# A gated recurrence and a PReLU layer on one core: gate factors folded, two chains made tasks of their own, and a new order of all instructions

## The chip, the core and the metric

The kernel runs on one core of a Trainium2 chip. The core has five engines with a queue of instructions each: TensorE (PE, with its weight loads as PEld), VectorE (DVE), ScalarE (ACT), GpSimd (POOL) and SyncE (SP), which here issues all transfers between the chip's memory (DRAM) and the core's memory. An engine takes its instructions in the order in which the program lists them; between engines, semaphores make one wait for another. The metric is the time of one execution on the device in microseconds (us); lower is better.

## The reference

Two layers follow each other. The first is a linear recurrence with a complex gate for each of 4 batches and 8 heads, over 768 tokens, with 48 channels; the second takes its output as 3072 tokens of 384 values.

```python
mag = np.sqrt(a_re * a_re + a_im * a_im)
scale = np.minimum(mag, 0.999) / (mag + 1e-06)
a_re_n, a_im_n = (a_re * scale, a_im * scale)
for t in range(S):
    ar, ai = (a_re_n[:, :, t, :, None], a_im_n[:, :, t, :, None])
    new_re = ar * S_re - ai * S_im
    new_im = ar * S_im + ai * S_re
    kv = np.einsum('bhd,bhe->bhde', k[:, :, t], v[:, :, t])
    S_re, S_im = (new_re + kv, new_im)
    y[:, :, t] = np.einsum('bhd,bhde->bhe', q[:, :, t], S_re)
...
h = x @ w_in
g = np.maximum(h, 0.0) + alpha * np.minimum(h, 0.0)
return (g @ w_out).astype(np.float32)
```

In the second layer w_in is 384 x 2048 and w_out 2048 x 384. All arithmetic of the kernel is in 32-bit floats; w_in, w_out arrive in 64 bits and are narrowed in the kernel.

## The kernel before, in words

The recurrence is not run token by token. A gate value is split into its magnitude, capped at 0.999 (the "decay"), and a number of length one (the "phase"). The products of phases up to each token turn q and k, so that inside a chunk of 128 tokens only real decays are left.

**Gates (`gates`, L229 to L516).** The work is cut into nine groups: the first batch's six chunks as 1, 2 and 3, each later batch as 3 and 3. A group of three chunks is a tile of 128 rows with six rows of 1152 columns, called x, c, f, d, e, y; the first group has 384 columns and is computed in halves, the second has 768. The steps for one group are: load a_re into x and a_im into y (L255); squares on ScalarE and their sum on VectorE (L263 to L269); reciprocal roots on ScalarE with a correction step on VectorE (L272 to L289); ScalarE's scaling of the magnitude c (L291); two products that turn x and y into the unit number (L363); the capped decay, written over rows d and e (`dec`, L380); copies that put the unit number into an order by place in blocks of eight tokens (`unit_numbers`, L344 to L358: the imaginary part, the real part and the negated imaginary part on ScalarE). Then the decay tree (L391 to L397): six levels of products of neighbouring decays, from 64 per chunk down to 2, the small ones on GpSimd from the fourth group on; then the transfer of the decays to a DRAM buffer, `decs` (L401). Then the running products of the unit numbers (`product`, L412 to L419: two VectorE instructions, L416 and L418, per step, in three rounds within blocks of eight, blocks of sixty-four and between those), one Newton step that brings their length back to one (L486 to L494), and the final product of each token's number with its block's (L507, L510), which overwrites the decay rows and is sent to a DRAM buffer, `phs` (L502, L512).

**Chunks (`unit`, L724 to L953).** There are 24. For each one q and k (`KQ`), the phases (`PP`), the decays with their tree (`T`) and v (`V`, `VL`) are loaded. VectorE turns q and k (L742, L744) and multiplies them by decays level after level (L797). TensorE makes the scores of six levels (`ps_lv`, L759), from copies that ScalarE puts in order (L820, L836). Then follow two transposes of k (L868), the update of the state from k and v (`ps_kv`, L880; state `St`, L916 on ScalarE and L918 on VectorE), the outputs inside the chunk (`ps_y`, L900), and those from the state (L930). ScalarE copies the sum out (L944), and it goes to DRAM (L949) and back as columns (`xT`, L962).

**The second layer.** `features` (L970) multiplies by w_in on TensorE (L978), ScalarE and VectorE make the PReLU (L985, L987); `outputs` (L992) multiplies by w_out (L997). The last three groups of tokens use a form with seven products in place of eight (L1097, L1172). The 64-bit weights are narrowed in `to_f32` by all of ScalarE (L588 to L592), GpSimd (L596) and VectorE (L598, L600).

**What sets the order.** Each of these is a Python generator, a task, that yields once ahead of each piece of work. The string `ORDER` at the top has one letter per step; `Plan.run` resumes the task of that letter and so writes its next instruction (or few) into the queues of the engines. The order of every queue is therefore fixed by that string, within the order inside each task. Buffers are single or few: V and VL one each, PP one, T two, KQ three, the gate tile two.

Of the kernel before, what the change touches and what calls it, by code (L numbers as in the profile page):

```python
# [9 lines left out]
F32 = mybir.dt.float32  # L10
# [8 lines left out]
P = 128  # L19
# [11 lines left out]
    "AAJMMAABAJAAAAAAAAAAAAAAAAAAAAMMMBJMAAAAAAAAAAKANAOAAAABAAANAAAKANNNABAMAJNBKOAKBOOKAABMAKABAAALOAAB"  # L31
    "LAKNOLNAALBOLANNAALBBLAAKBAKBBAKABABKMAAKBAAOAABAAAAAABABBABAAABAOOABABMANAAAAAAABAAAKBABNABBNBNOBOC"
    "BOCBJNNBLBOJBBOONBBNBBOCBBPBCBPPJLJMJCLKBNBCMBCJBPLBPCBOPPJCPBBBPOBPPBBNBPBBNNBBCPPMLPBLBBPLKBPKBCCC"
    "PLOKBKBPKBBBBCBPKCOOPKBPPPCPBPBCBPPPPBBPBCBBPBBPBBPBPCBPMPBCCBCBPNBKLCCNLCNPCPOCOJDCNDPPPJCOJNNCCCNJ"
    "OCNOOLCNOPCNKOMNNCPQPDJCQDLCDNQPPDQQQLCDQDKQQMCLNDQDOKPQQMODQLOOJQJDKQJDOLCQnOJOLDDJQNJOQLQLOOoLoDDC"
    "QLoQRQoLQQLQooooQQCoQDKNJooooRoMQoQCRCCoooooQoRDQQQCODDCONNCooRQRLoDCLRoMoLoCRRLCoooooCJoRDKCRKooooo"
    "RCDoRQLCDLCoooCoRKoOLCDJCQDCCoLDCRRDDCooooooLCQCooCLCoCoCoLCLCCCLCRCCLCKOCRCRLoCooCRRRCRRoRRCoCRCQQC"
    "CRCQCCoRKCRQRQQCQOORRoRCCQCCooRRCNQDoLoDLoNoDNoooNDoEDNNoEOJoDJRJDRLoooooDDoLDRRRLDRRLRDNDNEJDJSDDRo"
    "oJDESDEDSRDRJESSnJSoLESDoLoLODJSSJDSDLLTSDJoELoooooSSSDLoLooooJSSoDDDoSEDLoooSToSoJooJSSSDoSSDSSoooo"
    "ooSTSDETooooTToSEEoEDoooooSDToSEDTSESSSSDooLDTLoooLEEDSLToLSLoooooDLELoTJDSSSDoooooTTSDSESSSLoDooooo"  # L40
    "SEEDTLLoTKoooooDDDToTEJLDDDDoooooTEUJTDKoDoooKTToDoLoToooTLoUoDJoTLToooToEJoDonooToDEoDTKoUoDJooToUo"
    "EoEUTUEoETEDDDJTooUooDoUUoDooToToTTDoLoLoULoLDULLoooUUoDoLooooDoULoLoELooooLoUULoTLUTLJoooooFUEUoETT"
    "TUUUUTTTUooooTToUETUUFEoUEooooEoUVoUEoooooVVKJJUUEUUEUUoFooLEFLoUoLEUFJVUELoVJoUJooooVJEoFVEJEVoEUoo"
    "oUUUEVoEUoLoVVLEoooEoLEoVEJooooJVEWoFEnVVLoVELoLoooEoKVVEoELVEoJFooooJWoVoVFooWLooLVVEEWoLWVoLWVEFJV"
    "VVJEooVoVoooEKoWKoJEoooVEWWooVWoVoEFWVVVEVVEWELWEELooFEELoWLEoEoLoWWLVLoWEEEEVLLooooooLWEWLEoLEFELEK"
    "FFVVVooWooLooVVVVVFFFVLXKEoEWooooooEWWEEWWJoWWJoooWoEJWoWJoFJWoEWFFWWWWoEoELoLEoJoLoEoFXEooooFooooXo"
    "ooooKXWXLXFWoXoGGXLoXooooJWoLXoLWoFWXoXWFXWoFWXFWWoWXoXFFoFLoXoGFJFnGooooXXoJFoFLoLXXXXLGFLoooooXLFX"
    "XXoGoLFGFLoooooooFXoooGFoJoYJXoJFoJXFGKoooXFYFXoXFYJFooooGXXXYoYXLYFooLXFYFKoLoYoYLXXFZLFXLoXYXFLoXX"
    "XoooYXoFGLGFYYLoYGoFJoYFYJoooFoFZoLFoJoYJGKooooFJGYFYLooYYYLoJYYZGLLFoooooZLoFGYZYZoYZYKJFZZooooYFoZ"
    "YoYFGZYYFYFFYYFZFLFZFFLoYLoooZLooLoFFFFFYFZLFZYYYLFoZLYYFLYoooFZYLaZFLoFoooZZZZoYZZLZoGYFFLLoooZoZGo"  # L50
    "LGoFZJoZFFFGJoooooFooZFFZZFZZZGLoonoFLooLaoFoLoooaJoLoZoaJGoLZooaJaGoaoHoLZZLaaZoHGGoGZGZGGaZLGaLooo"
    "ooaZGaLoaJoZaZaooooGJoHaooHGoooaoaGLaHoooLoGLaaJaHoaJaaJoooooHoGbaoaGHoooaoGaobbJKHoaGaoaoaGaaHoLKoG"
    "JoboLGobLGoLGoooGbLoHGHbLboJbHoGJLaoLbbGLooooGoGHobLGaLaHbLGbabLaabaaGoLaooooLGbboGoGHbGooooJbGbGGKo"
    "bbboJobJbGGbcbbJobGGoooboGcbooooGbGoHbGbGcbbbLGcGLoooGbLcGHcGGJoboJcoLJGGGobLGccLGoobKcbLobHLbobbLoc"
    "obHoGHGdbLGHooooccocGoJoJHoooLcocdJooLconJHLoooocLcHoccccoccLGoJdcGGooocodHocHoHdHoHcGGGcoooGooocGGc"
    "GccccodGLLoooGcodooooLoddJoooLocdoLoIHIoHLdooooLHooLHdcoLdcoLdcLocJHcocddoHoHooKcoooILdocoLHoIHdcdLH"
    "LddoIKdooooJdoIddJoddKdHoHooodoHdoIoHedHHodeHIdddodoHLeHLoLoIHodLHoHLHeIHoLdLoooeeJHeHLoLdddHoooeeoH"
    "JHdedHLoJooooeIoLIeLeoeJddoLHoooLeeoLoHdIHeodJoHIHoooeeoJeeeeoeJeoeIJeoenJHIHoooeJIoeooHeHoHfeeoeHfe"
    "eoLLHoHHJHoHHeHoLfeoLILJHHHHofLooooofeLHfeHfLeHKoeIeLoKffLeHoooooefHeoeLgIIfogJLooooIoooffofoHJILooo"
    "ooHLffoJIoJfHHoooooKHofofJooLfffffofKoJgooHofgIoooggoIHIofofHIoIIoofoHKfooHofogfffoffggoLHLoLogoLoHI"  # L60
    "oLgoooILofnoIfgLgLgLfffoLggJoLgfKoooofooooIgLogfooLfIfofggggggogoohgogIhhLJJJIIhIooooogogoIIoogggggg"
    "oLILogoJIoJgIohJgIILgIgooohLIIgoJgIoIghILhIoIghILoLhhIooooIoIhIoJoLihILJooohhohLoLohLohoooLioJIIoLho"
    "LoJiJooohohooJhhiohhihJhihnoIIIhIoIIhIIIIooohIoIhIioIhihhhhhIihoLihLLLohhhLIIIIIiooooLohhiILiIoLiILo"
    "hLoooiiIoLohihohoLIoooILiIiLoLiiiiiioJioJioIIiIoooioiojoioIiiijIiiJooLojLoJoIoJoLjoooiLoIioLojIjiiiI"
    "jiiooooojjooooLojLiiJoooojLopoLjojiiLoooJjoLoojjJLojLLoooooJojLojooJjjjjjJojjJopjojookkkoojojooojjkj"
    "jojjokLkoLkLokJokoLokLoLoookLjooLjkJkokLLokkLoooLokooooLojjjLokjkjojkjjkojkkLlkookkopkJokJpoookokook"
    "oklkkkkLkLoookJlooLoLolooJokJopoJoLllJklnkLllokoooooklolokooollkkLLLolkoololoooJoLloJoLoooLlmlololoo"
# [1193 lines left out]
```

## Time and profile before

| | us |
|---|---|
| three runs | 821.32, 823.86, 829.38 |
| median | 823.86 |
| profiled execution | 820.38 |
| its span from first to last instruction | 818.6 |

| engine | busy us | instructions |
|---|---|---|
| TensorE matmul | 681.1 | 11680 |
| VectorE | 693.9 | 1191 |
| ScalarE | 520.3 | 1307 |
| GpSimd | 222.2 | 293 |

How to read what follows. A line of a group or of a timeline names engine, line of the kernel, operation, the tile written and the tiles read, and the shapes (partitions x elements). In a timeline the two numbers ahead are the start and the duration. A line of waits reads: engine, tile and line that waited, what it waited for, then the total in us, how often, and the longest. A line of stretches gives the length, then busy time and instructions of PE, PEld, DVE, ACT and POOL, the clock granted to TensorE, the share of the transfer engines' time and GB/s. The slices cut the span in 40 equal parts, and each digit is a busy share in tenths. "Places" of the SP queue count its 754 transfers from 0.

### The profile page before, as it was taken

Reading aid. Unit: us, or ns where it says so; the run is one execution under the profiler, and the core shown is the slowest. Engines: PE = TensorE matmul, PEld = TensorE weight load, DVE = VectorE, ACT = ScalarE, POOL = GpSimd, SP = SyncE. Lnnn points to the kernel's source line nnn. Section 1 sums busy time; section 2 is a strip of 40 time slices with the busy share of each in tenths; the row PEclk is TensorE's granted clock in tenths of the full one; section 3 lists DMA queues with packets and bytes.
Section 4 is the critical chain, followed back from the end, with each engine's and each line's share of the span. In section 5 each row is a group of like instructions: output and inputs, shape, how many; then the busy total and the mean of one; then the engine's idle time right before and its main releaser. Section 6 shows DMA issues by size and latency. Waiting matters only on the chain.

```text
span 818.6 us, 27870 instructions
## 1 busy us (share of the span) xinstructions
PE 681.1 (83%) x11680; PEld 539.0 (66%) x11680; DVE 693.9 (85%) x1191; ACT 520.3 (64%) x1307; POOL 222.2 (27%) x293
## 2 busy tenths in 40 slices
PE   0003128659998999999999999999999999999997
PEld 0003126537776777767777777777777777899997
DVE  5999999999989899999999989998787775456574
ACT  8777998669666777876876697555756544312121
POOL 7231343051604310531245054003200000233342
PEclk9999659979999999999999999999999999999999
DMA  8594895593689589738865867787566622101000
GB/s 242 176 294 128 266 296 158 177 253 101 182 235 197 140 194 272 174 90 279 195 168 141 253 160 180 223 197 184 117 182 134 153 77 56 44 1 40 1 21 20
DMA packets 186598, 130.99 MB, mean 160 GB/s; under 512 B 74728, under 2 KB 176872, under 8 KB 186088
## 3 DMA queue, kind: packets, MB, share of 16 engines
q1 hardware_dynamic: 186472, 129.20, 59.3%
q8 instruction: 92, 1.51, 0.8%
q14 instruction: 34, 0.28, 0.1%
HBM read 100.82 MB, written 35.71 MB: 167 GB/s over the span
## 4 chain that ended last, share of the span: by engine, by line
PE 65%; DVE 14%; DMA 10%; ACT 4%; SPq 2%; issue 2%; POOL 1%; DVEq 0%; ACTq 0%; POOLq 0%
PE ps_o L997 19%; PE ps_h L978 18%; PE ps_m L1172 7%; PE ps_lv L759 5%; PE ps_y L1097 4%; PE ps_h L1097 4%; PE ps_y L900 3%; DVE KQ L797 2%; PE ps_kv L880 2%; PE ps_y L930 2%; DMA VL<-in_v_dram 2%; DVE gate L507 2%; PE ps_kt L868 1%; DVE gate L416 1%; DMA T<-decs 1%
## 5 line engine op out<-in xcount | busy, mean ns | idle before, releaser
L978 PE MATMUL ps_h<-xT,w_in_sb 128*128 128x256 f32 (+1 forms) x960 | 227.0, 369 | 2.1 <-DVE w_in_sb L600 1.6
L997 PE MATMUL ps_o<-w_out_sb,g_sb 128*128 128x384 f32 x576 | 222.1, 501 | 4.8 <-DVE g_sb L987 4.7
L978 PEld LDWEIGHTS ps_h<-xT,w_in_sb 128*128 128x128 f32 x960 | 170.9, 195 | 51.3 <-DVE w_in_sb L600 2.2
L797 DVE TENSOR_TENSOR KQ<-KQ,T 96x1024 f32<-96x1024 f32 x120 | 148.4, 1237 | 25.8 <-PE ps_lv L759 19.2
L997 PEld LDWEIGHTS ps_o<-w_out_sb,g_sb 128*128 128x128 f32 x576 | 102.5, 191 | 44.9 <-DVE g_sb L987 6.5
L985 ACT ACTIVATE g_sb<-ps_h 128x256 f32<-128x256 f32 (+1 forms) x160 | 57.9, 362 | 73.0 <-PE ps_h L978 72.2
L759 PE MATMUL ps_lv<-WQ 96*32 96x32 f32 x2304 | 34.4, 203 | 83.6 <-DVE WQ L742 70.2
L759 PEld LDWEIGHTS ps_lv<-WQ 96*32 96x32 f32 x2304 | 26.3, 116 | 105.9 <-DVE WQ L742 71.0
L916 ACT ACTIVATE St<-St,T 96x48 f32<-96x48 f32 x352 | 84.0, 325 | 4.6 <-DVE St L918 4.3
L987 DVE SCALAR_TENSOR_TENSOR g_sb<-g_sb,al,ps_h 128x256 f32<-128x256 f32 (+1 forms) x160 | 71.3, 446 | 13.7 <-ACT g_sb L985 13.1
L1160 POOL TENSOR_TENSOR sums<-g_sb 128x128 f32<-128x128 f32 x48 | 21.8, 475 | 185.5 <-DMA VL<-in_v_dram 110.6
L416 POOL TENSOR_TENSOR gate<-gate 128x72 f32<-128x72 f32 x42 | 34.5, 822 | 133.7 <-ACT gate L446 130.9
L596 POOL TENSOR_SCALAR top<-top 128x768 f32<-128x768 f32 x16 | 44.1, 2755 | 74.6 <-ACT top L588 63.2
L820 ACT COPY WQ<-KQ 96x1024 f32<-96x1024 f32 x48 | 50.0, 1041 | 18.9 <-DVE KQ L797 18.3
L416 DVE TENSOR_TENSOR gate<-gate 128x576 f32<-128x576 f32 (+5 forms) x84 | 50.7, 604 | 1.1
L900 PE MATMUL ps_y<-A,VL 64*48 64x64 f32 x2304 | 41.9, 220 | 4.4 <-issue 4.3
L900 PEld LDWEIGHTS ps_y<-A,VL 64*48 64x48 f32 x2304 | 39.0, 122 | 6.8 <-issue 6.7
L507 DVE TENSOR_TENSOR gate<-gate 128x1152 f32<-128x1152 f32 (+2 forms) x36 | 42.8, 1220 | 0.8 <-POOL gate L492 0.7
L1135 ACT ACTIVATE rl<-g_sb 128x256 f32<-128x256 f32 x24 | 10.0, 416 | 50.0 <-DVE g_sb L1128 50.0
L773 ACT ACTIVATE A<-ps_lv,columns 128x64 f32<-128x64 f32 x144 | 37.4, 336 | 6.2 <-PE ps_lv L759 5.9
L836 ACT COPY W<-KQ 96x512 f32<-96x512 f32 x48 | 30.8, 641 | 16.2 <-DVE KQ L797 8.7
L759 PE MATMUL ps_lv<-KQ,W 96*32 96x32 f32 x1536 | 24.7, 204 | 18.5 <-ACT W L836 17.4
(168 smaller groups left out, 1355.7 us busy)
## 6 DMA issues: line engine op xcount, KB each, us to landing
T<-decs SPq DMA_DIRECT2D x48, 384.0 KB
PP<-phs SPq DMA_DIRECT2D x24, 387.0 KB
KQ<-in_q_dram SPq DMA_DIRECT2D x48, 192.0 KB
decs<-gate SPq DMA_DIRECT2D x7, 1152.0 KB
phs<-gate SPq DMA_DIRECT2D x14, 576.0 KB
KQ<-in_k_dram SPq DMA_DIRECT2D x40, 192.0 KB
vsc<-in_v_dram SPq DMA_DIRECT2D x48, 144.0 KB
VL<-vsc SPq DMA_DIRECT2D x48, 144.0 KB
```

Of the source, the lines that this page charges most:

```text
L416: on(4 * k).tensor_tensor(out=m, in0=w[:, 1::-1].unsqueeze(2).to_broadcast([P, 2, 2, k]), in1=pairs_of(u), op=ALU.mult)
L507: TT(out=m[:, a], in0=U5[:, 1 + a], in1=turned(off3, o)[:, a].unsqueeze(1).unsqueeze(3).to_broadcast([P, L // 2, nb, 2]), op=ALU.mult)
L759: nc.tensor.matmul(t[64 * i + j:64 * i + j + HC // 2, p], lhsT=keys(n, g), rhs=queries(n, g), start=True, stop=True)
L797: nc.vector.tensor_tensor(out=x, in0=x if x0 is None else x0, in1=m, op=ALU.mult)
L900: nc.tensor.matmul(o, lhsT=Vp[h][64 * i:64 * i + 64, s, e_ * D:(e_ + 1) * D], rhs=a, start=False, stop=False)
L916: nc.scalar.activation(St[:, n], before[:, n], AF.Copy, scale=T[0:D2, n, TL - 4 + s:TL - 3 + s])
L978: nc.tensor.matmul(p, lhsT=w_in_sb[:, f // 2, kk, f % 2 * P:(f % 2 + 1) * P], rhs=x_of[m][:, kk], start=(kk == 0), stop=(kk == NK - 1))
L985: nc.scalar.activation(gt, p, AF.Relu, scale=-1.0)
L987: nc.vector.scalar_tensor_tensor(out=gt, in0=gt, scalar=al_1[:, f:f + 1], in1=p, op0=ALU.mult, op1=ALU.add)
L997: nc.tensor.matmul(sums[0], lhsT=gt[:, c * P:(c + 1) * P], rhs=w_out_sb[:, f], start=(f == 0), stop=(f == NF - 1))
L1097: nc.tensor.matmul(o, lhsT=lhs, rhs=rhs, start=(at in (0, 5)), stop=(at in (4, 8)))
L1172: nc.tensor.matmul(banks[k][:, half], lhsT=lhs, rhs=rhs, start=(j == 0 and half == 0), stop=(j == NF // 2 - 1 and at in (2, 3, 5, 6)))
```

## The change

Four things change together.

- The gate's factors are folded: x carries the scale of 2^16 from its first pass, the reciprocal root and the square take factors of 4 and 2, the correction is written with a negated product, and the decay takes its factor from the last ScalarE pass over f. ScalarE's scaling of c goes (L291, and L373 in the first group).
- The product that makes the real part writes straight into block order, so ScalarE's copy of it goes (one of the two at L355; one of three half copies per half at L351). The rows of the tile are assigned anew for this.
- The decay tree with its transfer, and the part of a chunk that transposes k and updates the state, become tasks of their own (`decay_tree`, `unit_state`). What a task does inside stays; its place among the others is now free. The instruction counts of TensorE, VectorE, GpSimd and SP stay; ScalarE has 19 fewer.
- The string `ORDER` is a new one, and with it the order of all five queues.

"No sums on TensorE" in the change's description names nothing that either program has.

```diff
-        x, c, f, d, e, y = [G[:, i] for i in range(6)]
+        f, e, x, d, y, c = [G[:, i] for i in range(6)]
...
-            nc.scalar.activation(x, x, AF.Identity, scale=1.5, bias=bias_tiny)
+            nc.scalar.activation(x, x, AF.Identity, scale=1.5 * GATE_SCALE, bias=bias_tiny)
             yield ACT(N)
-            nc.scalar.activation(c, x, AF.Square, scale=GATE_SCALE)
+            nc.scalar.activation(c, x, AF.Square)
...
-            nc.scalar.activation(d, c, AF.Abs_reciprocal_sqrt)
+            nc.scalar.activation(d, c, AF.Abs_reciprocal_sqrt, scale=4.0)
             t = yield ACT(N, t)
-            nc.scalar.activation(e, d, AF.Square)
+            nc.scalar.activation(e, d, AF.Square, scale=2.0)
...
-            TT(out=e, in0=e, in1=c, op=ALU.mult)
+            STT(out=e, in0=e, scalar=-1.0, in1=c, op0=ALU.mult, op1=ALU.mult)
             t = yield DVE(N, t)
-            STT(out=d, in0=e, scalar=3.0, in1=d, op0=ALU.subtract, op1=ALU.mult)
+            STT(out=d, in0=e, scalar=3.0, in1=d, op0=ALU.add, op1=ALU.mult)
...
-            nc.scalar.activation(f, f, AF.Identity, scale=ONE / 2.0, bias=bias_half)
+            nc.scalar.activation(f, f, AF.Identity, scale=-ONE / (1.5 * GATE_SCALE), bias=bias_half)
             ts = yield DVE(N, t)
             TT(out=c, in0=c, in1=d, op=ALU.mult)
-            ts = yield ACT(N, ts)
-            nc.scalar.activation(c, c, AF.Copy, scale=1.0 / (1.5 * GATE_SCALE))
...
-            for o, p in ((2, y), (1, x)):
-                tu = yield ACT(N, tx, *after)
-                nc.scalar.copy(U5[:, o], by_place(p))
-            tu = yield ACT(N)
+            if C < 3:
+                yield ACT(N, ty)
+                nc.scalar.copy(U5[:, 2], by_place(y))
+            tu = yield ACT(N, *after)
             nc.scalar.activation(U[:, 0], U[:, 2], AF.Copy, scale=-1.0)
...
-            for p, w in ((x, -0.5), (y, -0.75)):
-                tx = yield DVE(N, t)
-                STT(out=p, in0=p, scalar=w * GATE_SCALE, in1=d, op0=ALU.mult, op1=ALU.mult)
+            ty = yield DVE(N, t)
+            STT(out=y, in0=y, scalar=1.5 * GATE_SCALE, in1=d, op0=ALU.mult, op1=ALU.mult)
+            tx = yield DVE(N, t)
+            TT(out=U5[:, 1], in0=by_place(x), in1=by_place(d), op=ALU.mult)
+            if C > 2:
+                ti = yield ACT(N, ty, tx)
+                nc.scalar.copy(U5[:, 2], by_place(y))
...
-                yield DVE(N, t, sent)
+                yield DVE(N, t, ("T", b * NCH + c0))
                 TT(out=m[:, a], in0=U5[:, 1 + a], in1=turned(off3, o)[:, a].unsqueeze(1).unsqueeze(3).to_broadcast(
...
+    def decay_tree(g, b, c0, c1):
+        C = c1 - c0
+        tiny, tiny_engine = (DVE, nc.vector) if g < 3 else (POOL, nc.gpsimd)
+        at = 0
+        t = ("dec", g)
+        while at < TL - 4:
+            m = (TL - at) // 2
+            k = NK * C * m // 2
+            t = yield (tiny if k <= SMALL else DVE)(k, t)
+            dec = dec_of[g]
+            pairs = dec[:, :, at:at + m].rearrange("p m (n s) -> p m n s", s=2)
+            (tiny_engine if k <= SMALL else nc.vector).tensor_tensor(
+                out=dec[:, :, at + m:at + m + m // 2], in0=pairs[:, :, :, 0], in1=pairs[:, :, :, 1], op=ALU.mult)
+            at += m
+        t = yield DMA(NK * C * P, t)
+        nc.sync.dma_start(scr_of[b * NCH + c0][0].rearrange("(t p) c s -> p t (c s)", p=P),
+                          dec.rearrange("p (t c) s -> p t (c s)", t=NK))
...
+        for u in range(NU):
+            plan.add(unit_state(u))
+        for i, g in enumerate(GATES):
+            plan.add(decay_tree(i, *g))
         plan.run(ORDER)
```

`unit_state` holds the former lines L864 to L882 and L904 to L923 of `unit` word for word, apart from the names by which the two tasks hand each other the state. In the first group (384 columns, not shown) the same edits are made on halves; there the product for y now stands ahead of the one for x, and ScalarE's copies of a half wait for the one for y.

More of the change, by code (lines that the diff above doesn't have):

```diff
@@ L370, in gates @@
             tf = yield ACT(N)
[L371 to L373 removed]
+            nc.scalar.activation(f, f, AF.Identity, scale=-ONE / (1.5 * GATE_SCALE), bias=bias_half)
+            ts = ts[1]
         if 0 < g and C < 3:
@@ L516, in gates @@
         done["gates", g] = used
+    dec_of = {}
+    def decay_tree(g, b, c0, c1):
[15 more added lines that the diff above has]
+                          dec.rearrange("p (t c) s -> p t (c s)", t=NK))
+        for u in range(b * NCH + c0, b * NCH + c1):
+            done["T", u] = t
     w_in_sb = consts.tile([P, NF // 2, NK, 2 * P], F32, tag="w_in_sb")
@@ L863, in unit @@
         last = c + 1 == NCH
[L864 to L882 removed]
+        done["stepped", u] = k_
+        T, V = L["T"], None
         for s in range(2):
@@ L901, in unit @@
                                              rhs=a, start=False, stop=False)
[L902 removed]
+        for name in (1, 4, 16, 32):
             R[name].put(ev)
[L904 to L923 removed]
+        v_used(u, ev)
         g, cg = group_of[u]
         for s in range(2):
[L927 to L928 removed]
+            e = yield PE(0.47, q_, ("known", u, s), mode=1, n=8)
+            before = before_of[u][s][0]
             for n in range(H):
```

262 lines of the change are left out of this document (132 added, 130 removed).

## The prediction

> **What bounds the kernel now.** I read four views in this order: the busy table with its slices, the sums by stretch, the waits of each engine, and the timeline where a wait stood out.
>
> ```profile
> PE 681.1 (83%) x11680; PEld 539.0 (66%) x11680; DVE 693.9 (85%) x1191; ACT 520.3 (64%) x1307; POOL 222.2 (27%) x293
> ...
> PE   0003128659998999999999999999999999999997
> ...
> DVE  5999999999989899999999989998787775456574
> ```
>
> ```profile
> 0.00:240.00 240.00, 113.96 (x2496) 90.15 (x2497) 224.96 (x415) 186.15 (x390) 80.34 (x76) 0.89 0.73 206
> 240.00:400.00 160.00, 154.71 (x2849) 115.84 (x2851) 148.79 (x214) 121.83 (x306) 40.75 (x50) 1.00 0.77 200
> 400.00:680.00 280.00, 278.20 (x5270) 208.27 (x5260) 243.89 (x353) 177.59 (x502) 58.17 (x71) 1.00 0.64 164
> ```
>
> The reader is to see two stages. Up to about 240 us VectorE (third number, 224.96 of 240) is full and TensorE (first number) idles for 240 - 113.96 = 126 us. From 240 to 680 us TensorE loses only 160 - 154.71 + 280 - 278.20 = 7 us. TensorE has the same matmuls in both programs (5984 in the program's order), so the time is TensorE's work plus what it loses, and nearly all of the loss lies in the VectorE stage. A gain must come from VectorE reaching the unit products earlier there.
>
> The waits of VectorE, from 0 to 20 us and from 225 to 255 us:
>
> ```profile
> DVE gate L305 <- ACT gate L303: 4.3, 2, 3.6
> DVE gate L380 <- ACT gate L373: 2.5, 1, 2.5
> ```
>
> ```profile
> DVE WQ L742 <- issue: 2.8, 1, 2.8
> DVE KQ L797 <- DMA T<-decs: 1.3, 1, 1.3
> ```
>
> Between them VectorE waits under 3 us in all: the queue is gapless. What is left to gain there is in the spacing of its instructions:
>
> ```profile
> 32.93 0.17 DVE L416 TENSOR_TENSOR gate<-run,runs 128x12 f32<-128x12 f32 x1
> 33.13 0.17 DVE L418 TENSOR_TENSOR run<-gate 128x6 f32<-128x6 f32 x1
> ...
> 35.75 0.21 DVE L488 TENSOR_TENSOR gate<-gate 128x48 f32<-128x48 f32 x1
> 35.88 0.35 DVE L396 TENSOR_TENSOR gate<-gate 128x192 f32<-128x192 f32 x1
> 36.15 0.18 DVE L490 TENSOR_SCALAR gate<-gate 128x48 f32<-128x48 f32 x1
> ```
>
> L418 uses what L416 just made: it starts 0.20 us after a start of 0.17 us, so 0.03 us after its end. L488, L396 and L490 belong to two chains: each starts 0.08 us before the one ahead has ended. Over all of the trace the medians are +0.034 us for an instruction that waits for the one directly ahead and -0.079 us for the rest. So a dependent neighbour costs 0.113 us.
>
> **The change part by part.**
>
> *VectorE's work.* 1191 instructions in both programs. Two forms change: the product L279 (1359 ns) becomes a three-operand one like L281 (1422 ns), +0.06 us on each gate; the one that makes the real part (L363, 1381 ns) becomes a product with a block-order output like L510 (1352 ns), -0.03 us. Four gates lie in the VectorE stage: +0.1 us, taken as 0.
>
> *VectorE's order.* I added the row times of the instructions ahead of the first step of each unit (L797 on WQ) in both orders. Ahead of unit 1: 87.5 us before, 87.6 after; unit 2: 111.4 and 111.3; unit 3: 155.0 and 155.9; unit 4: 168.5 and 168.5; unit 5: 193.9 and 193.5. TensorE's work ahead of the first matmul of the first, second and third group of features: 8.8 and 8.1, 42.2 and 42.2, 74.0 and 74.3 us. So the new order puts the same work ahead of the same milestones: 0, bounds -0.4 to +0.9 us.
>
> *Dependent neighbours.* With the trees apart from the products, VectorE has more to put between two steps of one chain. Ahead of unit 3's first product 82 instructions wait for their direct neighbour before, 61 after: 21 x 0.113 = -2.4 us. Upper bound 0, if the queue only reaches a transfer sooner (unit 0's product waits 1.1 us for PP already). I take -2.4, since VectorE is otherwise gapless.
>
> [...]
>
> *ScalarE.* Per whole gate two passes go: the scaling L291 (1161 ns) and one of the copies L355 (1275 ns). Seven gates of 1152 columns give 8.1 + 8.9 us, the one of 768 columns 0.8 + 0.9, the first gate two half copies and L373: 20 us in all. In the VectorE stage ScalarE is ahead of VectorE (no wait on it after 20 us longer than 0.3 us), so there this is worth 0, except at the start: the first decays (L380) wait 2.5 us for a ScalarE chain of six half copies (L351, 0.28 us apart) and L373 (0.51 us). Two copies less, L373 gone, and the copies waiting for the first product and not the second (0.3 us): -1.2 us, bounds -1.4 and 0. Later, where TensorE waits for ScalarE's copies, bounds 0 and -4 us (over half of the 7 us that it loses); I take 0, because the order of TensorE's own queue changes with them and no row says which of these waits would go.
>
> *The SP queue.* The transfer of the decays (decs<-gate) was fixed behind its tree in the gate's own sequence; now it stands later: of the fifth gate at place 262 of SP's 754 instead of 214, of the third at 139 instead of 85.
>
> ```profile
> SPq L401 <- POOL gate L396: 5.2, 1, 5.2
> SPq L512 <- DVE KQ L797: 1.2, 1, 1.2
> ```
>
> These are SP's waits from 210 to 225 us. For 5.2 us SP stood at the fifth gate's tree, then issued without a break until PP of unit 6 at 237.3 us, for which L742 waited 2.8 us. At place 262 the tree is long done, so that wait goes: 0 to -2.8 us. TensorE was full from 220 to 240 us and lost 2.3 us in the next 20, so I take -1.5. The 1.3 us wait for T stays: it follows T's ring, through ysc<-T.
>
> *A new wait.* The last products of a gate (L507) overwrite the decay rows, so they wait for that transfer to land. For the third gate it now stands behind the V and VL loads of unit 2, 17 places after w_out's last load, which was issued at 133.4 us; SP issues one in 0.65 us here: 133.4 + 11.0 = 144.4 us. The nearest landings are 5.5 us (T<-decs) and 9.5 us (KQ at 98 us), giving 150 to 154 us. L507 ran at 150.5 us, and would be ready at about 147 with the gains above; but the SP loads ahead are released by TensorE and ScalarE, which come earlier too, by up to 3.6 us. Stall: 0 to 6.5 us on VectorE; behind it wait the eight final products and sums of that gate, PP of unit 3 and unit 3's first matmuls. I take +1.0, nearer to the 5.5 us landing, because DMA is busy for 0.52 to 0.58 of the time there and not 1.10. The other gates have 4 us or more between place and use.
>
> *Sum.* -2.4 - 1.2 - 1.5 + 1.0 = -4.1 us. The profiled execution took 820.4 us (span 818.6 and 1.8 around it): 816.3. The median of the three runs, 823.9, stood 3.5 us above it, so a median like it would be 819.8 us, 0.5% faster.
>
> **The rivals.**
>
> *A larger gain.* ScalarE's 20 us count. For it: between 100 and 120 us it is busy for 18.7 of 20 us, and TensorE's largest waits after the first are for its copies (17.4 us on L836, 13.4 on L820). Against it: those lie where VectorE paces everything. With -2.4, -1.4, -2.8, the -4 later and no stall: 820.4 - 10.6 + 3.5 = 813.3 us.
>
> *Slower: the late decay transfer.* One place, SP 139. If it lands in 9.5 us, at 154 us, the stall is 6.5 us: -5.1 + 6.5 = +1.4, 825.3 us. If SP also waits for V's release ahead of it as long as at its worst in this trace (L681 on L880, 5.9 us), it lands near 160, the stall is 12.8 and PP of unit 3 goes with it: -5.1 + 12.8 = +7.7, 831.6 us; with the second gate's transfer, whose slack is 4 us, slower by over 1%. It decides from a landing 5 us behind L507's turn.
>
> [...]
>
> **How the numbers follow.** The forecast has 0.43, the larger gain 0.22, nothing left 0.13, the late transfer 0.22, of which 0.12 beyond 1%. About 1% (8 us) is what a measurement of this kernel can tell from no change. Faster 0.22, same 0.43 + 0.13 + 0.10 = 0.66, slower 0.12. The forecast's own range is 816 to 823. The range of 8 in 10 goes from 811 (the larger gain with 2 us of spread) to 830 (the late transfer almost in full).
>
> **What would show it.** VectorE's wait at L380 near 13 us falls to about 1.3 us, and L742 of unit 0 starts 2 to 3 us before 52.9; L742 of unit 3 starts near 168 instead of 172.4 us. No SP wait for a tree of 5 us near 217 us, and L742 of unit 6 without a 2.8 us wait. TensorE's busy time in the first 240 us rises from 114 by about 3 to 4 us, and stays 7 us short of full from 240 to 680. Wrong would be: VectorE waiting for decs<-gate at its last products, above all near 147 us; VectorE's share in the first 240 us under 93%; TensorE losing over 12 us after 240.

## The result and the profile after

The changed kernel takes 832.8 us (median of 8 runs, 831.0 to 836.2), the kernel before 824.2 us on the same chip (8 runs, 821.3 to 829.4): ratio 1.0103, 95% interval 1.0072 to 1.0134. It is slower by 1%, where 819.8 us was predicted, and lies outside the range of 811 to 830 us. The profiled span grew from 818.6 to 831.5 us, by 12.9.

Line numbers move in the changed kernel: the V load L681 is L700, w_out's rows L572 are L591, the decays' transfer L401 is L532, the narrowing L588 is L607, the final products L507 are L503, the products of q and k L742 are L761, the transposes of k L868 are L955, the state matmuls L880 are L967, the decay tree L396 is L528, the steps of the running products L416 and L418 are L412 and L414, the score matmuls L759 are L778, ScalarE's ordering copies L836 are L855, and the PReLU's L985 and L987 are L1024 and L1026.

The page of the changed kernel, busy times and slices:

```profile
PE 690.1 (83%) x11680; PEld 546.4 (66%) x11680; DVE 691.1 (83%) x1191; ACT 501.7 (60%) x1288; POOL 214.7 (26%) x293
...
PE   0004048659998999999989999999999999999997
...
DVE  6999996899979999899988998998786867455574
```

The same stretches as shown of the kernel before:

```profile
0.00:240.00 240.00, 115.69 (x2462) 91.52 (x2464) 217.83 (x407) 172.76 (x366) 84.54 (x76) 0.86 0.71 196
240.00:400.00 160.00, 151.81 (x2788) 113.28 (x2778) 145.46 (x211) 111.85 (x295) 34.71 (x47) 1.00 0.75 194
400.00:680.00 280.00, 275.54 (x5079) 206.74 (x5080) 239.25 (x340) 177.08 (x501) 53.23 (x74) 0.99 0.69 174
```

VectorE's share of the first 240 us fell from 94% to 217.83 / 240 = 91%: the queue that was gapless has gaps now. TensorE loses 8.2 + 4.5 = 12.7 us after 240, where it lost 7. The same matmuls keep it busy for 9.0 us longer (690.1 against 681.1), and it idles for 3.9 us more. The longer busy time fits the lower clock of the first part (0.86 against 0.89): by the clock records of the two traces TensorE works 34.4 us at a granted 0.50, against 17.6 before. In the changed kernel's timeline 48 matmuls of `ps_y` (L902) take 1.49 us at a granted 0.50 (at 123.98 us) and 0.89 at the full clock (at 129.40), two of `ps_o` (L1036) 1.65 and 0.91 (at 125.99 and 130.22). By these, the 16.8 us more at 0.50 are 6.8 to 7.5 us of longer work, an estimate.

Where the time goes is read from the first score matmul of a unit (`ps_lv`, start in us). The last column is the changed order with three places mended (all three together, below).

| | before | after | difference | mended |
|---|---|---|---|---|
| unit 0 | 54.1 | 52.1 | -2.0 | 52.5 |
| unit 1 | 100.4 | 93.7 | -6.7 | 93.8 |
| unit 2 | 130.9 | 125.4 | -5.5 | 126.1 |
| unit 3 | 173.7 | 175.4 | +1.7 | 167.9 |
| unit 4 | 191.0 | 196.6 | +5.6 | 189.2 |
| unit 6 | 251.4 | 259.6 | +8.3 | 249.6 |
| unit 12 | 405.3 | 413.2 | +7.9 | 403.0 |
| unit 13 | 425.4 | 439.1 | +13.8 | 425.7 |
| end of span | 818.6 | 831.5 | +12.9 | 819.7 |

The gain is there, up to unit 1. It is lost in three places, as far as these starts tell; what each is worth is for the experiments to say.

**First place, 120 to 155 us.** The timeline of the kernel before, unit 1's state and the V load of unit 2 (start, duration):

```profile
122.85 0.85 PE L868 MATMUL ps_kt<-ident,KQ 96*128 96x96 f32 x4
...
127.78 1.15 PE L880 MATMUL ps_kv<-V,T 64*64 64x48 f32 x64
128.99 0.34 SPq L681 DMA_DIRECT2D V<-in_v_dram  x1
133.44 0.39 SPq L572 DMA_DIRECT2D g_sb<-in_w_out_dram  x1
...
142.27 0.52 SPq L401 DMA_DIRECT2D decs<-gate  x1
```

The timeline of the changed kernel, the same work:

```profile
119.66 0.61 SPq L591 DMA_DIRECT2D g_sb<-in_w_in_dram  x1
...
122.47 0.90 PE L955 MATMUL ps_kt<-ident,KQ 96*128 96x96 f32 x4 [0.91 <-DVE KQ L816]
...
135.91 1.15 PE L967 MATMUL ps_kv<-V,T 64*64 64x48 f32 x64
...
137.14 0.34 SPq L700 DMA_DIRECT2D V<-in_v_dram  x1
...
137.58 0.44 SPq L591 DMA_DIRECT2D g_sb<-in_w_out_dram  x1
...
143.59 0.89 ACT L607 ACTIVATE top<-g_sb 128x768 f32<-128x768 f32 x1 [5.57 <-DMA g_sb<-in_w_out_dram]
...
144.91 0.35 DVE L1026 SCALAR_TENSOR_TENSOR g_sb<-g_sb,al,ps_h 128x128 f32<-128x128 f32 x1 [5.53 <-ACT g_sb L1024]
...
148.84 0.37 SPq L532 DMA_DIRECT2D decs<-gate  x1
```

Read it from the state matmuls. As a task of their own they follow the transposes by 13.4 us, where it was 4.9. V has a single buffer, so its next load waits for them, and SP takes its queue in order: it issues nothing from 120.3 us, the end of its last issue, to 137.1 us. Behind V stands a row of w_out that nothing of this chain needs. It lands at 143.6; ScalarE waits for it, VectorE for ScalarE. The decays of the third gate leave SP only at 148.8 us, where it was 142.3. The waits of the changed kernel in that stretch say the same (engine, tile and line, what it waited for, total, times, longest):

```profile
DVE g_sb L1026 <- ACT g_sb L1024: 6.0, 2, 5.5
...
ACT top L607 <- DMA g_sb<-in_w_out_dram: 5.6, 1, 5.6
```

SP's own wait for V from 118 to 160 us, in the kernel before and in the changed one, and VectorE's wait for the landing of the decays in the changed one:

```profile
SPq L681 <- PE ps_kv L880: 5.1, 1, 5.1
...
SPq L700 <- PE ps_kv L967: 16.8, 1, 16.8
...
DVE gate L503 <- DMA decs<-gate: 1.7, 1, 1.7
```

Over the whole kernel, SP waits for state matmuls 70.7 us in place of 39.1.

**Second place, 222 to 250 us.** SP stands 6.2 us for V behind the state matmuls of unit 4, which start at 228.6 instead of 217.9 us. PP of unit 6 is issued at 243.5 us, and VectorE waits for it, 4.6 us where it was 2.8:

```profile
DVE WQ L761 <- issue: 4.6, 1, 4.6
```

**Third place, 408 to 437 us.** ScalarE's copy of the seventh gate's runs waits for GpSimd's small products, and the transposes behind it hold TensorE:

```profile
ACT runs L440 <- POOL gate L414: 5.2, 1, 5.2
...
PE ps_kt L955 <- ACT T L958: 2.6, 1, 2.6
```

### The profile page after: what moved, and what is told of

It reads as the page before. It is cut to its first block, busy times and chain, and to the rows that moved or that the text cites. A ratio compares the mean times of both kernels' runs of the same rounds, so it can differ in the third digit from the quotient of the medians.

```text
span 831.5 us, 27814 instructions
## 1 busy us (share of the span) xinstructions
PE 690.1 (83%) x11680; PEld 546.4 (66%) x11680; DVE 691.1 (83%) x1191; ACT 501.7 (60%) x1288; POOL 214.7 (26%) x293
## 4 chain that ended last, share of the span: by engine, by line
PE 58%; DVE 16%; DMA 11%; ACT 6%; POOL 4%; issue 3%; SPq 2%; DVEq 0%; ACTq 0%; POOLq 0%
PE ps_o L1036 16%; PE ps_h L1017 15%; PE ps_m L1211 6%; PE ps_lv L778 4%; DVE KQ L816 4%; PE ps_y L1136 3%; PE ps_h L1136 3%; PE ps_y L902 3%; DMA T<-decs 2%; PE ps_y L912 2%; DMA phs<-gate 2%; PE ps_kv L967 2%; DVE gate L412 2%; DMA ysc<-T 2%; DVE gate L503 2%
## 5 line engine op out<-in xcount | busy, mean ns | idle before, releaser
L1036 PE MATMUL ps_o<-w_out_sb,g_sb 128*128 128x384 f32 x576 | 224.7, 505 | 8.7 <-DVE g_sb L1026 8.6
L1017 PEld LDWEIGHTS ps_h<-xT,w_in_sb 128*128 128x128 f32 x960 | 173.1, 196 | 58.6 <-DMA xT<-ysc 5.6
L1036 PEld LDWEIGHTS ps_o<-w_out_sb,g_sb 128*128 128x128 f32 x576 | 103.0, 192 | 49.0 <-DVE g_sb L1026 10.5
L1024 ACT ACTIVATE g_sb<-ps_h 128x256 f32<-128x256 f32 (+1 forms) x160 | 57.7, 361 | 82.7 <-PE ps_h L1017 81.9
L778 PE MATMUL ps_lv<-WQ 96*32 96x32 f32 x2304 | 34.6, 204 | 74.7 <-DVE WQ L761 65.3
L1026 DVE SCALAR_TENSOR_TENSOR g_sb<-g_sb,al,ps_h 128x256 f32<-128x256 f32 (+1 forms) x160 | 71.4, 446 | 22.5 <-ACT g_sb L1024 22.1
L778 PEld LDWEIGHTS ps_lv<-WQ 96*32 96x32 f32 x2304 | 26.4, 116 | 95.1 <-DVE WQ L761 65.6
L615 POOL TENSOR_SCALAR top<-top 128x768 f32<-128x768 f32 x16 | 50.3, 3152 | 57.2 <-ACT top L607 54.4
L412 POOL TENSOR_TENSOR gate<-gate 128x72 f32<-128x72 f32 x42 | 30.0, 713 | 117.8 <-ACT gate L442 115.1
L412 DVE TENSOR_TENSOR gate<-gate 128x576 f32<-128x576 f32 (+5 forms) x84 | 49.2, 585 | 0.8
L778 PE MATMUL ps_lv<-KQ,W 96*32 96x32 f32 x1536 | 24.8, 204 | 27.3 <-ACT W L855 27.0
L902 PE MATMUL ps_y<-A,VL 64*48 64x64 f32 x2304 | 43.7, 229 | 0.7 <-issue 0.7
L855 ACT COPY W<-KQ 96x512 f32<-96x512 f32 x48 | 30.7, 640 | 22.4 <-DVE KQ L816 18.4
L503 DVE TENSOR_TENSOR gate<-gate 128x1152 f32<-128x1152 f32 (+2 forms) x36 | 42.6, 1217 | 1.7 <-DMA decs<-gate 1.7
L902 PEld LDWEIGHTS ps_y<-A,VL 64*48 64x48 f32 x2304 | 41.2, 129 | 2.1 <-issue 1.6
L528 POOL TENSOR_TENSOR gate<-gate 128x72 f32<-128x72 f32 (+2 forms) x18 | 11.7, 651 | 118.6 <-DVE gate L528 118.0
```

Of the source, the lines that this page charges most:

```text
L412: on(4 * k).tensor_tensor(out=m, in0=w[:, 1::-1].unsqueeze(2).to_broadcast([P, 2, 2, k]), in1=pairs_of(u), op=ALU.mult)
L503: TT(out=m[:, a], in0=U5[:, 1 + a], in1=turned(off3, o)[:, a].unsqueeze(1).unsqueeze(3).to_broadcast([P, L // 2, nb, 2]), op=ALU.mult)
L615: nc.gpsimd.tensor_scalar(out=top, in0=top, scalar1=F64_SMALL, scalar2=None, op0=ALU.max)
L778: nc.tensor.matmul(t[64 * i + j:64 * i + j + HC // 2, p], lhsT=keys(n, g), rhs=queries(n, g), start=True, stop=True)
L902: nc.tensor.matmul(o, lhsT=Vp[h][64 * i:64 * i + 64, s, e_ * D:(e_ + 1) * D], rhs=a, start=False, stop=False)
L1017: nc.tensor.matmul(p, lhsT=w_in_sb[:, f // 2, kk, f % 2 * P:(f % 2 + 1) * P], rhs=x_of[m][:, kk], start=(kk == 0), stop=(kk == NK - 1))
```

## The experiments

The theory is what these places say: late state matmuls hold SP at V, and what stands behind V comes late. The rivals: the folding of the gates costs it; TensorE's lower clock costs it; the passes taken from ScalarE count for more than nothing. A ratio is against the kernel before on the same chip, with its 95% interval. In the cuts of `ORDER` below a letter is one step of a task, and a number is its place in that string.

### Folded gates, every queue in the old order

```diff
 gates: folded factors as in the change
-ORDER of the change
+ORDER of the kernel before, written for the new tasks
```

> The changed gates (factors folded, product in block order, 19 passes less on ScalarE), with every queue in the order that the kernel before had. Theory 1 (the new order alone makes the kernel slower): 820 to 824 us, as before or up to 3 us faster, with the early transfers and unit 2 where they were: V of the third unit on SP near 129 us. Theory 2 (the fold itself costs, by its product with a block-order output or by a wait on ScalarE's copy): 828 us or more.

825.9 us, 1.005 (1.0021 to 1.0079): a little slower, no gain. The start comes 0.55 us earlier, and the waits of VectorE before 60 us show where that goes:

```profile
DVE WQ L761 <- DMA St<-in_v_dram: 2.7, 1, 2.7
...
DVE gate L385 <- ACT gate L377: 1.9, 1, 1.9
```

L761 of unit 0 waits 2.7 us for its transfers (1.1 before), and the scores of unit 0 start 2.4 us later than in the kernel before. The time lies between the two ranges: with the old order the folded gates cost 0.2 to 0.8%, so the folding may hold a part of the 1%, but not all of it. The 20 us taken from ScalarE give no gain in the old order.

### The first place mended in steps

One w_out row ahead of the V load:

```diff
-...QosQLRRM...
+...QosQMLRR...
```

> The changed kernel, with one transfer moved: the w_out rows that SP issued at 137.6 us, behind its 16.8 us wait for V, are issued ahead of that wait. Theory 1 (SP's queue passes the wait for the state matmuls on): the 5.6 us wait of ScalarE and the 5.5 us wait of VectorE at 139 to 145 us go, but the third gate's decay transfer is still behind V (landing near 155 us), so VectorE waits some 7 us for it at its last products (1.7 us now): 831 to 834 us, no gain. Rival (the w_out rows alone are what is late): 826 to 828 us.

832.8 us, 1.0103 (1.0061 to 1.0144). As expected, no gain: the next thing behind V holds VectorE instead. Waits of this kernel, 118 to 160 us:

```profile
DVE gate L503 <- DMA decs<-gate: 6.2, 1, 6.2
```

The row, and the third gate's decays with it, ahead of the V wait (seven loads of V and VL go behind):

```diff
 steps of ORDER
-  L at 551, M at 554, * at 642
+  M at 551, * then L at 590
```

> The changed kernel, with the same w_out rows and the third gate's decay transfer issued ahead of SP's wait for V; the state matmuls of the second unit stay where they are on TensorE. Theory 1: both waits of VectorE go (5.5 and 1.7 us), unit 3 starts near 168 us instead of 175.4, and the run takes 825 to 828 us. Rival (the late state matmuls on TensorE themselves set the time, whatever SP does; or the lower TensorE clock from 100 to 220 us does): 831 to 834 us.

826.7 us, 1.005 (1.0019 to 1.0081). Unit 3 starts at 167.3 us, 8.1 earlier than in the changed kernel. VectorE then waits 6.5 us for PP of unit 6, at the second place. TensorE's queue is as it was: the state matmuls of unit 1 are as late as in the changed kernel (135.2 us, 135.9 there) and the granted clock is the same (0.958, 0.957 there). So about half of the loss was neither the late matmuls themselves nor the clock, but what stood behind V.

The other way round, unit 1's state early and SP's queue as it is:

```diff
 unit_state(1), steps 2 to 9
-  at 549 563 577 599 600 635 640 688
+  ahead of 526 529 536 544 566 572 600 611
```

> The changed kernel, with the second unit's transposes, state matmuls and state updates back where the order before had them (state matmuls near place 322 of TensorE's instead of 450); no transfer is moved on SP. Theory 1: V is released near 129 us and not 137, SP's wait falls from 16.8 to some 9 us, the w_out rows land near 136 and the decays near 147: 825 to 828 us, like the run with both transfers moved. Rival (clock): 831 to 834 us.

830.2 us, 1.0093 (1.0061 to 1.0126): short of what was expected. V is issued at 129.7 us and unit 3 starts at 171.6 us, 3.8 earlier, but SP then waits 8.7 us for ScalarE's first phases of the third gate (L498), and PP is late at units 3 and 6 (VectorE waits 1.5 and 3.4 us). By the ratios it can't be told from the changed kernel.

### All three places

Unit 4's state earlier as well:

```diff
 unit_state(4), steps 4 to 9
-  at 1107 1126 1130 1159 1174 1185
+  ahead of 1076 1092 1115 1119 1146 1148
```

> The run with the w_out rows and the third gate's decays moved, and with the state matmuls and state updates of the fifth unit 60 places earlier on TensorE as well. Theory 1 (the same mechanism at 222 us: SP stands 6.2 us for V, then issues the last products and PP of unit 6 late, for which VectorE waits 6.5 us): the wait for PP falls under 2 us and the run takes 822 to 825 us (826.7 without). Rival (VectorE has slack there, or TensorE is full and the wait costs nothing): 826 to 828 us.

824.1 us, 1.0013 (0.998 to 1.0047), as expected; the wait for PP of unit 6 is 1.0 us. That is 0.4% under the run without this step (1.005), which the two intervals together do not tell from nothing. The third place by itself, ScalarE's two copies later:

```diff
-  G at 2278 and 2288
+  G ahead of 2297
```

> The changed kernel, with two small ScalarE copies of the seventh gate (runs<-gate) behind the copies A<-ps_lv of unit 12 and not ahead of them; all other queues as they were. Theory 1 (a second place where the new order makes a queue stand: at 424.5 us ScalarE waits 5.2 us for POOL's small rows, TensorE then 2.6 us for ScalarE): 827 to 830 us. Rival (TensorE is short of work there anyway, or the wait comes back at once at the transfer of T or PP): 831 to 834 us.

833.8 us, 1.0123 (1.0082 to 1.0164): a miss. The wait of 5.2 us is gone, and others stand in its place (waits of this kernel, 400 to 445 us); SP waits 6.1 us for V there as well:

```profile
ACT W L855 <- DVE run L414: 3.3, 1, 3.3
...
PE ps_lv L778 <- ACT W L855: 2.8, 1, 2.8
DVE WQ L761 <- DMA PP<-phs: 2.7, 1, 2.7
```

All three together:

> All three places mended: the changed kernel with the w_out rows and the decays ahead of SP's wait, the fifth unit's state matmuls earlier, and the two small copies of the seventh gate behind unit 12's. Theory 1: what the new order gained by unit 1 (6.7 us earlier) is kept, and the run is faster than the kernel before, 816 to 821 us. Rival (other waits take their place): 822 to 826 us.

821.7 us, 0.9995 (0.9966 to 1.0023): level with the kernel before, and 1.1% under the changed one by the two ratios. Its stretches:

```profile
0.00:240.00 240.00, 119.01 (x2502) 93.90 (x2502) 224.44 (x417) 178.33 (x385) 76.86 (x76) 0.87 0.75 207
240.00:400.00 160.00, 154.19 (x2904) 116.16 (x2905) 149.31 (x217) 115.04 (x296) 33.31 (x49) 1.00 0.74 191
```

VectorE is back at 224.44 of 240, and TensorE does 5 us more in the first 240 us than before. So the place of one row, of one transfer, of one unit's state and of two copies makes up the loss, within the interval. The first place gives about half (1.0103 to 1.005, 0.5% with an uncertainty of 0.4 by the two intervals); the other two together give the rest (1.005 to 0.9995), and which of them does is open: the third alone gave nothing, and behind the other two it gives 0.2%, again within the intervals. The forecast's gain does not come back with the waits mended. Unit 3 starts 5.8 us ahead of the kernel before, unit 13 0.3 us behind it. TensorE idles 135.3 us in all, 2.2 less than in the kernel before, but is busy 3.3 us longer (684.4), at a clock of 0.963 and not 0.968. With unit 13's phases and decays also ahead of the V wait near 408 us:

```diff
-  J at 2184 2208 2232 2259
+  J ahead of 2159
```

> All three places mended, and the loads of q, k and PP of unit 13 issued ahead of SP's wait for V at 408 us (they stood behind it; VectorE waits 2.5 us for that PP at 416 us). Theory 1 (SP's wait for V is what makes later loads late, here too): the 2.5 us wait goes and the run takes 818 to 821 us. Rival (TensorE is full there and absorbs it): 821 to 823 us.

822.7 us, 0.9988 (0.9958 to 1.0018). The wait of 2.5 us for PP there is gone; in its profile VectorE waits 3.1 us for ScalarE near by. No difference from the three places. No version here beats both kernels by more than the measurement's spread.

### The reverse: a late state in the old order

```diff
 the folded kernel in the old order; unit_state(1), steps 1 to 5
-  at 509 512 524 526 536
+  ahead of 559 566 577 581 591
```

> The folded gates in the old order (825.9 us), with one thing made late: unit 1's two transposes of k, their copies and the state matmuls stand about 60 of the order's letters later, as late against unit 2's scores as in the changed kernel. Nothing else moves. Theory (the late state matmuls hold SP at the V load, and the w_out row and what follows behind it): SP's wait for V near 131 us grows from under 1 us to 5 to 10 us, ScalarE and VectorE wait 3 to 5 us for that w_out row near 143 us, and the time is 829 to 832 us, near the changed kernel. Rival (the state's place costs nothing by itself, only the new order as a whole does): 825 to 827 us.

837.4 us, 1.0171 (1.0133 to 1.0209), where the same kernel without this move took 825.9. That is above the theory's range. SP waits 15.5 us for V (6.0 in the kernel it starts from), and from 118 to 160 us ScalarE waits for the w_out row and VectorE for ScalarE, as in the changed kernel, though at another line:

```profile
SPq L700 <- PE ps_kv L967: 15.5, 1, 15.5
...
ACT top L607 <- DMA g_sb<-in_w_out_dram: 4.9, 1, 4.9
DVE gate L412 <- ACT runs L442: 4.0, 1, 4.0
```

Unit 3 is 4.5 us later, as the theory has it. The other 6 to 7 us come after 290 us, from something else, which the runs with spare matmuls show too: pauses of TensorE for which the profile names no cause, 12.5 us of them here and 4.0 in the kernel that this one starts from (the position of TensorE's instructions, below). So of the 11.5 us the theory explains some 4.5.

### ScalarE's passes given back

```diff
+            nc.scalar.activation(c, c, AF.Copy, scale=1.0)
...
+                nc.scalar.copy(U[:, 1], U[:, 1])
```

These and three like them add the 19 passes to the changed kernel, in their old places and without an effect on the values.

> The changed kernel with ScalarE's 19 passes given back (a scaling by 1 and an in-place copy in each gate, some 20 us of ScalarE), at the places of the old ones; all other queues as they were. By the forecast's term (ScalarE's 20 us are worth 0 but for the start): 833 to 836 us. Rival (ScalarE's passes count, as in the forecast's case of a larger gain): 838 us or more.

848.8 us, 1.0322 (1.0274 to 1.0369): 16 us above the changed kernel. VectorE's waits for ScalarE at L1026 (L1031 in this kernel) grow from 22.1 to 35.3 us, SP's for state matmuls from 70.7 to 83.3. Its profiled execution is one of its slowest, 23.3 us longer than that of the changed kernel. In it 8.7 us are stops of TensorE of the kind that the next experiments show (0.7 in the changed kernel), so 15.3 of the 23.3 us are something else. How the 16 us of the medians divide is not known. So ScalarE's passes count in the new order, though no gain from them was seen in the old one.

### Spare matmuls against the low clock

TensorE's granted clock is 0.50 from 90 to 110 us, where TensorE is busy for 2.6 of 20 us, as the stretches below show (the traces of both kernels have no clock record for their first 80 us). The stretches of the changed kernel, 90 to 130 us (length, busy times, then the granted clock as the third number from the end):

```profile
90.00:100.00 10.00, 0.65 (x32) 0.52 (x32) 10.00 (x16) 6.47 (x8) 6.61 (x2) 0.50 1.08 319
100.00:110.00 10.00, 1.96 (x96) 1.56 (x96) 9.62 (x13) 9.71 (x13) 6.88 (x2) 0.50 0.93 246
110.00:120.00 10.00, 4.14 (x76) 3.66 (x76) 9.54 (x11) 9.89 (x14) 5.36 (x1) 0.57 0.77 178
120.00:130.00 10.00, 8.89 (x177) 7.00 (x181) 8.97 (x13) 5.50 (x14) 4.51 (x3) 0.66 0.59 154
```

To see whether that costs time, the gaps were filled with matmuls that nothing reads, ahead of the work that ends each gap:

```diff
+            for _ in range(n):
+                nc.tensor.matmul(o, lhsT=ident[:, 0:D], rhs=ident, start=True, stop=True)
```

> The changed kernel with 374 spare matmuls (128x128, on the identity, into a tile that the next real matmul overwrites), put where TensorE stood idle for over 1.5 us between 50 and 440 us, to fill 85% of each gap; every other queue as it was. It asks what the lower TensorE clock costs (granted 0.5 to 0.8 between 80 and 190 us; TensorE's busy time 690 us, 661.6 by full-clock rows). Theory 1 (the waits set the time there, the clock little): 829 to 833 us. Rival (clock: most of the 9 us that TensorE is busy longer than before is lost to the clock and on the path): 822 to 827 us.

> The kernel before with 335 such spare matmuls in its own gaps, as a control. Theory 1: 821 to 825 us, no change beyond 2 us. Rival (clock): faster by the same few us as the changed kernel with spare matmuls, 815 to 820 us, in which case the clock explains none of the difference between the two kernels.

> The run with all three places mended, with 341 spare matmuls in its gaps. Theory 1: 820 to 823 us, as without. Rival (clock): 813 to 818 us.

The changed kernel takes 864.5 us so (1.0458, 1.0396 to 1.0519), the kernel before 852.6 (1.0347, 1.0295 to 1.0399) and the mended one 852.8 (1.0352, 1.0296 to 1.0409). All are outside both ranges. The mean clock rose to 0.98, but one spare matmul took 0.28 us (26 of them 7.33 us from 52.91 us on, in the changed kernel), where the filling had allowed 0.16 (85% of the 69.7 us of gaps for 374), so they filled more than the gap. With a third as many:

> The changed kernel with spare matmuls in TensorE's gaps again, 135 in place of 374, each costed at the 0.29 us that the last ones took and filling 0.6 of a gap. Theory (the clock that falls after a gap costs time by itself): granted clock above 0.957, TensorE's needed matmuls back near 681 us, and 3 to 8 us less than the changed kernel, 825 to 830 us, with the same kernel before gaining less (3 us or under). Rival (the low clock only accompanies the waits; VectorE sets the pace there): 831 to 835 us, no gain. Above 838 us the spare matmuls are again in the way, and it stays open.

> The control: the kernel before with 121 spare matmuls in its own gaps, sized the same way. If the clock costs time: 820 to 823 us. If it does not: 823 to 827 us. Above 829 us the spare matmuls are in the way.

> The changed order with its three places mended (822 us), with 120 spare matmuls sized the same way. If the clock costs time: 816 to 820 us, which would be faster than the kernel before. If it does not: 821 to 825 us. Above 828 us the spare matmuls are in the way.

In the same order 852.4 us (1.0342, 1.0305 to 1.038), 846.0 (1.0277, 1.0234 to 1.032) and 840.2 (1.021, 1.0176 to 1.0244), at a mean clock of 0.959, 0.960 and 0.962 in the profiled executions, where it was 0.957, 0.968 and 0.963 without spare matmuls. The control is slower by 22 us, and little of that comes where the spare matmuls stand: its units 0 to 5 start 1.4 to 2.1 us late, unit 6 4.9 us, unit 16 18.6 us, long after the last spare matmul at 178 us. All three times lie above the bounds beyond which the question was to stay open: what the low clock costs by itself is not settled by these runs.

### The position of TensorE's instructions

The late loss has one form: TensorE stands still, and the profile gives no wait (issue). The page of the kernel before lists 92 transfers that bring instructions (queue, kind, count, MB, share of 16 engines' time):

```profile
q8 instruction: 92, 1.51, 0.8%
```

Each has 16 KB, and the trace has 23636 weight loads, matmuls and semaphore instructions of TensorE, 257 for each transfer. Count TensorE's weight loads, matmuls and semaphore instructions from the start of its trace, and take the pauses of over 0.5 us that the profile gives no wait for. In the kernel before they lie 7424, 768, 4608 and 4608 instructions apart, all multiples of 256; so counted in blocks of 256, each falls at one place, 192, by the author's count in every run, and in the kernel before and the changed one it ends 1.2 to 1.7 us after the end of such a transfer. The kernel before has 5 of them (4.9 us of standing still), the changed one 1 (0.7), the mended one 3 (3.0), the late state in the old order 7 (12.5), the kernel before with 121 spare matmuls 13 (25.0). The author took this for a queue that had run dry, which no view shows directly. To test it, spare matmuls stand only at the head of the old kernel's queue, where TensorE idles to 54 us:

```diff
+FILL = {257: 40}    (58 in the second)
```

> The kernel before, order untouched, with 40 spare matmuls at the head of TensorE's queue, where it idles until 52 us. They shift all of TensorE's later instructions by 159 places. Theory: TensorE's instructions come in transfers of 16 KB, 256 at a time; in all runs so far its stops that no wait explains fall on place 192 of a block, and a stretch of short matmuls just ahead of that place runs out before the next block has landed. From the rows of the kernel before, with its own latencies, a shift of 160 puts about 19 us more of such stretches there: 838 to 850 us, with 15 to 30 us of stops marked issue, all at place 192. Rival (the stops in the kernels with spare matmuls came from the matmuls' own place and the clock): 822 to 826 us.

> The same with 58 spare matmuls in place of 40, a shift of 231 places. By the theory this is a good position (by the same reckoning 5 us fewer stops than the kernel before itself): 818 to 824 us, though it holds more spare matmuls than the other. Rival: the same time as with 40.

845.5 us (1.0265, 1.0224 to 1.0305) and 839.9 (1.0199, 1.0163 to 1.0235). Both are slower than the kernel before: 11 stops at place 192 with 20.3 us in the first, 8 with 17.2 us in the second. Unit 0 is 1.1 us late in both, unit 7 is 2.5 us late and 0.4 us early; the rest comes behind it. The first was forecast; for the second a good position was forecast, and it is not: the reckoning by the latencies of one execution does not say which position is good. The mean clock is lower too (0.92, where it was 0.97). The slices of both pages have 0.5 to 0.6 from 21 to 126 us, and the kernel before has no clock record ahead of 83 us; from 190 us on they have 0.9 or more but for one of 0.8, from 569 us in the first and 565 in the second. So it is shown that 40 or 58 spare matmuls in idle time cost 23 and 17 us, nearly all of it long after them, and that the stops at place 192 come with it. That the position alone decides, and not the spare matmuls in some other way, is argued: a shift by a whole block of 256, which should change nothing, was not run. The timeline of the first, with 40 spare matmuls:

```profile
300.17 1.56 PE L912 MATMUL ps_y<-A,VL 64*48 64x64 f32 x95
305.81 0.25 PE L912 MATMUL ps_y<-A,VL 64*48 64x64 f32 x1 [4.08 <-issue]
306.00 2.81 PE L1010 MATMUL ps_o<-w_out_sb,g_sb 128*128 128x384 f32 x4
```

The kernel before, the same matmuls:

```profile
294.25 1.58 PE L900 MATMUL ps_y<-A,VL 64*48 64x64 f32 x96
295.76 1.56 PE L997 MATMUL ps_o<-w_out_sb,g_sb 128*128 128x384 f32 x4
```

The 96th of 96 equal matmuls stands 4.08 us, and the profile names nothing that it waits for. The changed kernel has 4.2 us less of these stops than the kernel before, so in these two executions they are no part of its loss.

Most blocks pass without such a stop (none of over 0.5 us at 87 of 92 in the kernel before), but not all: the longest is 5.5 us (ScalarE's passes given back), and in one execution they are 20.3 us in all (40 spare matmuls).

## Why the prediction was wrong

The steps, in its own order:

- **Start**: L380 came 0.9 us earlier (13.27 to 12.35), forecast 1.2; its wait fell from 2.5 to 1.9, not to 1.3. Unit 0's product starts at 50.8 us, 2.1 before 52.9, as forecast.
- **Dependent neighbours**: right in kind, about two thirds in size. Up to unit 3's first step, VectorE's spacing is 1.6 us shorter (forecast 2.4, to unit 3's first product). It led to nothing in the changed kernel, and in the mended one unit 3's product starts at 166.6 us, where 168 was forecast.
- **VectorE's and TensorE's order, 0**: this is the step that failed. The same VectorE work stands ahead of the same first steps, which was right, but it was the wrong sum. TensorE's queue was compared at the scores and features only, not at the state matmuls, which had become a task of their own and stand at 450 instead of 322 of its matmuls (unit 1). They release V, and V holds SP's queue. Up to unit 3, VectorE's waits grew from 9.6 to 17.3 us. With the w_out row and the decays taken from behind V the kernel is 0.5% slower than before and not 1%; with all three places mended it is level (0.9995).
- **TensorE's work, taken as the same**: the forecast reckoned the time as TensorE's work plus what it loses, and had no term for the work itself taking longer. The same matmuls took 9.0 us more of busy time, of 12.9 us by which the span grew. Whether this costs time by itself is open: with the row and the decays moved the granted clock is the same (0.958, 0.957 in the changed kernel), and half of the loss is gone.
- **A VectorE gain ahead of unit 3 is a gain of the kernel**: not borne out either. The mended kernel has it (5.8 us at unit 3) and is no faster than the kernel before.
- **A new wait**: the place was right (L503 waits for the third gate's decays), the size was close (1.7 us, +1.0 taken), and the rival that priced SP's wait for V at 5.9 us, its worst before, was right in its mechanism. That wait became 16.8 us. What decided first was not the decays, but the w_out row ahead of them, at 5.5 us of VectorE's time; no step looked at what else stands behind V.
- **The SP queue**: the wait for the fifth gate's tree went, as forecast. The gain did not come: a wait of 6.2 us for V took its place, and L761 of unit 6 waits 4.6 us, not less than 2.8.
- **ScalarE, 0**: no gain seen in the old order (825.9 us), as taken, but wrong as a rule: given back in the new order, the passes make it 3.2% slower than the kernel before, and not 1%. So taking them away hid part of what the new order costs; some of the difference is stops of TensorE (8.0 us in the profiled execution).
- **Forms and milestones**: 0.06 us and under 1 us, small, as VectorE's instructions up to unit 3 show: they take 0.8 us less in all.

All three signs that were named as wrong appeared: VectorE under 93%, TensorE losing 12.7 us, and the wait for decs at the last products, though with 1.7 us only.

What stays open: how much of the 9.0 us of longer busy time is a cost of its own, which of the second and third place gives the second half of the loss, what the folding costs in the old order, and how the 16 us of ScalarE's passes divide.

## What to carry to other kernels

When part of a task may move freely, look up which buffers that part releases, and which in-order queue waits for them; then list everything behind the waiting entry, above all what has nothing to do with it, and price the last of it. Equal work ahead of a milestone says nothing about a release that lies between two milestones. Ahead of reading a difference of 1 to 2% as the work of an edit, look for pauses without a wait on the engine with the most instructions: adding or moving a few may cost more than the edit (here 40 spare matmuls cost 22.8 us, the change 8.6).

## What the hardware showed that was not expected

- TensorE stands still without a wait in the profile: stops of 0.5 to 5.5 us, all at place 192 of a block of 256 instructions, and in the kernel before and the changed one 1.2 to 1.7 us after the end of a transfer of 16 KB. 40 spare matmuls in idle time cost 22.8 us, 58 cost 17.2.
- The clock granted to TensorE was 0.50 from 90 to 110 us of the changed kernel, with 2.6 us of work in 20. The work that began at 114.7 us had the full clock 3.9 us later; the clock fell again at 122.1 us, behind 1.64 us of work in 3.50, and stayed at 0.50 for 6.8 us in which TensorE was busy for 6.43 (stretches of TensorE alone: length, its busy time, then the clock):

```profile
114.70:118.60 3.90, 3.86 (x76) 0.50 1.09 258
118.60:122.10 3.50, 1.64 (x8) 0.99 1.20 243
122.10:128.90 6.80, 6.43 (x128) 0.50 0.49 143
128.90:132.00 3.10, 3.10 (x78) 1.00 0.02 5
```

  The second return to the full clock took 6.8 us, nearly twice as long as the first, 3.9.
